# Layer two's output products with weights as the stationary side, and PSUM dealt anew

## The chip, the cores and the metric

The kernel runs on one core of a Trainium2 chip. A core has TensorE (PE: matrix products, out of SBUF into PSUM), VectorE (DVE), ScalarE (ACT), GpSimdE (POOL), and queues that start transfers (SP here, mostly). PSUM has eight banks; one holds 512 fp32 columns on 128 partitions. The metric is device time in microseconds (us), the median of several runs.

## The reference, cut to what matters

```python
# x: (4, 8, 768, 32), a: (4, 8, 768), B and C: (4, 8, 768, 16), all fp32
for c in range(nc):                         # chunked linear attention with decay
    cum = np.cumsum(la, axis=-1)            # la = log(a) of the chunk
    L = np.exp(cum[:, :, :, None] - cum[:, :, None, :]) * causal
    y_intra = ((Cc @ Bc^T) * L) @ xc
    y_inter = (Cc @ state) * np.exp(cum)
    y[chunk] = y_intra + y_inter
    state = decay_full * state + (Bc * decay_from_j)^T @ xc
x = y as (3072 tokens, 256)
h = x @ w_in                                # layer one: (3072, 256) x (256, 2048)
g = where(h > 0, h, exp(min(h, 0)) - 1)     # elu
x = g @ w_out                               # (3072, 2048) x (2048, 256)
h = x @ w_in2                               # layer two, the same sizes
g = h * tanh(softplus(h))                   # mish
out = g @ w_out2
```

## The kernel before, in words

Tokens are ordered in 32 attention tiles of 96 tokens (a chunk of 96 here, four batches in turn), and the feed-forward layers go over seven blocks of 384, 384, 512, 512, 512, 512 and 256 tokens (BL). The two layers' blocks are interleaved in one list, `order`: (1,0), (1,1), (2,0), (2,1), (1,2), (1,3), (2,2), (1,4), (2,3), (1,5), (2,4), (1,6), (2,5), (2,6), as (layer, block). A block has 16 slots, one for each 128 of the 2048 hidden features.

fp32 precision comes from splitting an operand into a high and a low fp32r part, and three products hi x hi, hi x lo, lo x hi. For h (`emit_h`) a slot has six matmuls: two halves of the 256 inputs times three, weights as the stationary side (lhsT), tokens as the moving one (rhs), so h has features on partitions and tokens in columns. ACT and DVE make g from it (`elu_1` to `elu_3`, or `mish_1`), then its parts gh and gl (`split_hi`, `split_lo`).

Layer one's second product (`emit_y1`) keeps this layout: six matmuls a slot with the block's tokens as columns, into two banks, y transposed, which is what the next layer wants. Layer two's second product (`emit_y2`) has to give rows of tokens: gh and gl are the stationary side, 128 tokens at a time, and the weights move: for each 128 tokens one matmul of 512 columns (gh with hi and lo side by side) and one of 256 (gl with hi). A block of 512 thus has four such pairs a slot and four accumulator banks. At the block's end `y2_out1` (ACT or DVE) scales the second half, `y2_out2` (DVE) adds the first, and `y2_store` writes rows of 256 floats out.

PSUM before: pool `ph` two banks (tag h), pool `pa` two banks of tag acc and two of tag accb, pool `px` two banks (tag s, attention). Tag accb has the third and fourth accumulator of layer two, attention's first outputs (`new_ys`), and the odd slots' h of layer one (`h_other`).

The order of the work on each engine comes from a planner in the kernel itself. Every piece is a `step` with the engines that can do it, a cost in us, what it depends on, and perhaps a due time `dl`. Buffers are `Ring`s: `take` gives the next turn at a buffer, and turns are used in the order in which they were taken. `run_steps` simulates the engines, picks at each moment the ready step that is due first (due times run back through what depends on a step), and emits the instructions in that order. Engines then run in order, so a step that waits holds what stands behind it on its engine, SP's transfers too. `slot_time(s)` is the time at which slot s ought to start.

Attention's steps for a tile: loads (`load_bc`, `load_c96`, `load_x`, `at_cumrow`), bf16 parts (`three_parts`) turned by a DMA transpose (`at_split_5`), the decay mask (`at_diff`, `at_mask`, `at_exp`), scores (`at_scores`), their product with the mask (`at_p`), `at_y` and `at_st` on PE, and `at_y_hi` and `at_y_lo`, which write layer one's input. The first eight tiles use PE transposes (`at_tr0`) instead.

Of the kernel before, what the change touches and what calls it, by code (L numbers as in the profile page):

```python
# [18 lines left out]
def tile_chain(  # L19
# [25 lines left out]
    FP = 2  # L45
    NP = NF // FP
# [3 lines left out]
    WB, GB, HB = 3, 3, 2  # L50
# [9 lines left out]
    px = ctx.enter_context(tc.tile_pool(name="px", bufs=2, space=bass.MemoryType.PSUM))  # L60
# [45 lines left out]
    class Need:  # L106
# [9 lines left out]
        w=Ring(WB), gh=Ring(GB), gl=Ring(GB), h=Ring(HB), acc=Ring(2), accb=Ring(2), s=Ring(2), xy=Ring(3), x=Ring(5), bc=Ring(2),  # L116
        d=Ring(2), r=Ring(1), t=Ring(1), r1=Ring(1), bw=Ring(2), o=Ring(2), stk=Ring(1),
# [219 lines left out]
    def w_hi(key, k):  # L337
        return wt[key, k][:, 0]
# [4 lines left out]

    def job_1(j, eng):
# [430 lines left out]
    def h_other(s):  # L775

        layer, c, f = at_slot(s)
        return layer == 1 and f % 2 and (f >= 5 or s >= NF and order[s // NF - 1][0] == 1)

    def emit_h(s):  # L780
# [5 lines left out]
        p, t = (pa, "accb") if h_other(s) else (ph, "h")  # L786
        h = p.tile([128, MT], F32, tag=t, name="h")[:, 0:BL[c]]
# [496 lines left out]
```

## Time and profile before

| | |
|---|---|
| median of three runs | 613.85 us (613.49 to 615.1) |
| the profiled execution | 614.17 us, span of its instructions 612.1 us |
| mean granted clock of TensorE | 0.986 |
| PE, PE weight loads | 598.7 us, 506.4 us busy |
| DVE, ACT, POOL | 433.2, 377.4, 177.6 us busy |
| instructions | 10993, of them 3876 matmuls |
| read from and written to HBM | 32.31 MB, 3.24 MB |

How to read it: a matmul's end is modelled and overlaps the next one's start, so its duration is more than what it costs; the pace is the distance between starts. The profile names for each wait the event that came last. In a row such as `h<-xyh,wi 128*128 128x512` the tile written stands ahead of the arrow, then the tiles read, the stationary size, and the moving one.

### The profile page before, as it was taken

How to read it: one execution, taken by the hardware profiler on the slowest of the kernel's cores; microseconds unless marked ns; L12 is line 12 of the kernel's file. 1: busy time of each engine (PE TensorE's matmuls, PEld its weight loads, DVE VectorE, ACT ScalarE, POOL GpSimd, SP SyncE). 2: the span in 40 equal slices, each digit the busy share in tenths (PEclk: the TensorE clock that was granted, in tenths of full speed). 3: DMA queues.
4: the chain of work that ended last, by engine and by line, in shares of the span. 5: the costliest groups of instructions: out<-in, count | busy, mean ns of one | idle time of the engine just before them, and what ended most of it. 6: DMA issues, size and time to landing. Idle time of an engine off the chain costs nothing.

```text
span 612.1 us, 10993 instructions
## 1 busy us (share of the span) xinstructions
PE 598.7 (98%) x3876; PEld 506.4 (83%) x3876; DVE 433.2 (71%) x948; ACT 377.4 (62%) x705; POOL 177.6 (29%) x238
## 2 busy tenths in 40 slices
PE   6899999999999999999999999999999999999997
PEld 5677799999987878888878888878888888988896
DVE  5899899987887888765877766767764545744454
ACT  4699999976878775554786644597544214542121
POOL 2346455222556545100544301536100000200000
PEclk9599999999999999999999999999999999999999
DMA  7799894205564543002463302533300000000010
GB/s 149 190 244 297 260 260 103 56 9 99 104 121 85 111 81 68 5 0 52 72 114 73 80 1 27 104 82 74 62 0 1 1 0 19 19 1 0 1 36 18
DMA packets 133655, 47.09 MB, mean 77 GB/s; under 512 B 116672, under 2 KB 122432, under 8 KB 133600
## 3 DMA queue, kind: packets, MB, share of 16 engines
q1 hardware_dynamic: 133488, 46.29, 34.5%
q8 instruction: 30, 0.49, 0.4%
q14 instruction: 25, 0.20, 0.1%
q10 hardware_dynamic: 112, 0.10, 0.0%
HBM read 32.31 MB, written 3.24 MB: 58 GB/s over the span
## 4 chain that ended last, share of the span: by engine, by line
PE 92%; DMA 3%; ACT 2%; DVE 1%; issue 1%; SPq 0%; ACTq 0%; DVEq 0%
PE h L789 15%; PE h L790 14%; PE h L791 14%; PE acc L883 14%; PE acc L884 7%; PE acc L852 6%; PE acc L853 6%; PE acc L854 6%; PE acc L857 4%; PE ys L716 2%; DMA t<-stk 2%; PE s L667 2%; PE s L679 1%; ACT L836 1%; PE ys L746 1%
## 5 line engine op out<-in xcount | busy, mean ns | idle before, releaser
L789 PE MATMUL h<-xyh,wi 128*128 128x512 f32 (+2 forms) x448 | 168.5, 376 | 1.0 <-ACT w L836 0.9
L790 PE MATMUL h<-xyl,wi 128*128 128x512 f32 (+2 forms) x448 | 162.2, 362 | 0.2 <-DVE xyl L733 0.2
L791 PE MATMUL h<-xyh,wi 128*128 128x512 f32 (+2 forms) x448 | 162.0, 362 | 0.0
L883 PE MATMUL acc<-wo,gh 128*128 128x512 f32 x384 | 142.5, 402 | 0.0
L832 DVE TENSOR_TENSOR gl<-w,gh 128x512 fp32r<-128x512 f32 (+2 forms) x181 | 122.5, 678 | 21.5 <-ACT gh L375 12.9
L836 ACT ACTIVATE w<-h 128x512 f32<-128x512 f32 (+2 forms) x112 | 59.4, 536 | 100.9 <-PE h L791 68.7
L884 PE MATMUL acc<-wo,gl 128*128 128x256 f32 x384 | 107.5, 280 | 0.0
L377 DVE CAST gh<-w 128x512 fp32r<-128x512 f32 (+2 forms) x114 | 47.0, 414 | 74.8 <-PE acc L883 51.2
L789 PEld LDWEIGHTS h<-xyh,wi 128*128 128x128 f32 x448 | 85.0, 190 | 17.4 <-ACT w L836 2.5
L791 PEld LDWEIGHTS h<-xyh,wi 128*128 128x128 f32 x448 | 85.0, 190 | 10.7
L790 PEld LDWEIGHTS h<-xyl,wi 128*128 128x128 f32 x448 | 85.2, 190 | 9.7 <-DVE xyl L733 0.5
L883 PEld LDWEIGHTS acc<-wo,gh 128*128 128x128 f32 x384 | 72.2, 188 | 15.5
L805 ACT ACTIVATE w<-h 128x512 f32<-128x512 f32 (+2 forms) x96 | 51.7, 540 | 51.1 <-PE h L791 37.1
L884 PEld LDWEIGHTS acc<-wo,gl 128*128 128x128 f32 x384 | 72.5, 189 | 2.2
L832 POOL TENSOR_TENSOR gl<-w,gh 128x512 fp32r<-128x512 f32 (+2 forms) x27 | 29.6, 1096 | 147.6 <-ACT gh L375 95.6
L375 ACT ACTIVATE gh<-w 128x512 fp32r<-128x512 f32 (+2 forms) x94 | 54.9, 584 | 27.8 <-PE acc L853 23.4
L852 PE MATMUL acc<-gh,wo 128*128 128x512 f32 (+2 forms) x192 | 70.2, 365 | 0.0
L854 PE MATMUL acc<-gl,wo 128*128 128x512 f32 (+2 forms) x192 | 69.6, 363 | 0.0
L853 PE MATMUL acc<-gh,wo 128*128 128x512 f32 (+2 forms) x192 | 69.6, 362 | 0.0
L813 DVE TENSOR_SCALAR w<-w 128x512 f32<-128x512 f32 (+2 forms) x74 | 30.5, 414 | 26.2 <-ACT w L805 25.2
L595 POOL TENSOR_TENSOR d<-bc,dk 32x384 f32<-32x384 f32 x28 | 27.9, 999 | 68.8 <-DVE gl L832 41.8
L821 DVE TENSOR_TENSOR w<-h,w 128x512 f32<-128x512 f32 (+2 forms) x74 | 46.6, 631 | 1.5
(102 smaller groups left out, 821.4 us busy)
## 6 DMA issues: line engine op xcount, KB each, us to landing
d<-cum_d SPq DMA_DIRECT2D x31, 288.0 KB, 3.9
raw<-in_moe_w_in_dram SPq DMA_DIRECT2D x16, 512.0 KB, 6.5
raw<-in_moe_w_out_dram SPq DMA_DIRECT2D x16, 512.0 KB, 5.9
xs<-in_x_dram SPq DMA_DIRECT2D x32, 96.0 KB, 2.9
bc<-in_C_dram SPq DMA_DIRECT2D x32, 48.0 KB, 2.4
bc<-in_B_dram SPq DMA_DIRECT2D x32, 48.0 KB, 2.7
out_dram<-o SPq DMA_DIRECT2D x15, 96.0 KB, 1.9
bc<-bc SPq DMA_DIRECT2D x84, 16.0 KB, 2.4
```

Source lines behind the costliest of these rows:

```text
L375: nc.scalar.activation(out=out, in_=in_, func=AF.Copy)
L789: nc.tensor.matmul(out=h, lhsT=hi[:, k, fs], rhs=xh[:, k, :], start=(k == 0), stop=False)
L790: nc.tensor.matmul(out=h, lhsT=hi[:, k, fs], rhs=xl[:, k, :], start=False, stop=False)
L791: nc.tensor.matmul(out=h, lhsT=lo[:, k, fs], rhs=xh[:, k, :], start=False, stop=(k == 1))
L805: nc.scalar.activation(out=new_w(s), in_=st[s][0], func=AF.Exp)
L832: alu(eng).tensor_tensor(out=gl, in0=w, in1=gh.bitcast(F32), op=ALU.subtract)
L836: nc.scalar.activation(out=new_w(s), in_=st[s][0], func=AF.Mish)
L852: nc.tensor.matmul(out=y, lhsT=hi[:, f % FP, ds], rhs=gh, start=(f == 0), stop=False)
L853: nc.tensor.matmul(out=y, lhsT=lo[:, f % FP, ds], rhs=gh, start=False, stop=False)
L854: nc.tensor.matmul(out=y, lhsT=hi[:, f % FP, ds], rhs=gl, start=False, stop=(f == NF - 1))
L883: nc.tensor.matmul(out=y, lhsT=gh[:, ts], rhs=w[:, :, f % FP, :], start=(f == 0), stop=False)
L884: nc.tensor.matmul(out=y[:, 0], lhsT=gl[:, ts], rhs=w[:, 0, f % FP, :], start=False, stop=(f == NF - 1))
```

## The change

The diff, with the changed cost figures of the planner cut to a few:

```diff
@@ -43,11 +43,12 @@
     DFF = w_in1.shape[1]
     NF = DFF // 128
     FP = 2
+    EARLY = 20.0
     NP = NF // FP
     LAG = 5
     N0 = NF
     TR0 = range(2 * NB)
-    WB, GB, HB = 3, 3, 2
+    WB, GB, HB = 3, 3, 3
 
     const = ctx.enter_context(tc.tile_pool(name="const", bufs=1))
     wpool = ctx.enter_context(tc.tile_pool(name="wpool", bufs=1))
@@ -57,7 +58,7 @@
     at = ctx.enter_context(tc.tile_pool(name="at", bufs=1))
     ph = ctx.enter_context(tc.tile_pool(name="ph", bufs=HB, space=bass.MemoryType.PSUM))
     pa = ctx.enter_context(tc.tile_pool(name="pa", bufs=2, space=bass.MemoryType.PSUM))
-    px = ctx.enter_context(tc.tile_pool(name="px", bufs=2, space=bass.MemoryType.PSUM))
+    px = ctx.enter_context(tc.tile_pool(name="px", bufs=3, space=bass.MemoryType.PSUM))
     dram = ctx.enter_context(tc.tile_pool(name="dram", bufs=1, space=bass.MemoryType.DRAM))
 
     ctx.enter_context(tc.manual_schedule())
@@ -113,8 +114,8 @@
             return iter(self.free)
 
     rings = dict(
-        w=Ring(WB), gh=Ring(GB), gl=Ring(GB), h=Ring(HB), acc=Ring(2), accb=Ring(2), s=Ring(2), xy=Ring(3), x=Ring(5), bc=Ring(2),
-        d=Ring(2), r=Ring(1), t=Ring(1), r1=Ring(1), bw=Ring(2), o=Ring(2), stk=Ring(1),
+        w=Ring(WB), gh=Ring(GB), gl=Ring(GB), h=Ring(HB), acc=Ring(2), s=Ring(3), xy=Ring(3), x=Ring(5), bc=Ring(2),
+        d=Ring(2), r=Ring(1), t=Ring(1), r1=Ring(1), bw=Ring(2), o=Ring(2), stk=Ring(1), turned=Ring(1),
     )
 
     def take(name):
@@ -341,6 +342,14 @@
         return wt[key, k][:, 1]
 
 
+    def by_rows(key, w):
+        return w.rearrange("p k f (b q) -> p (f b) k q", q=32) if key == "o2" else w
+
+    def from_raw(key, r):
+        w = r[:, :, :, 1].bitcast(F32)
+        return w.rearrange("p f (b k q) -> p (f b) k q", k=2, q=32) if key == "o2" else w
+
+
     def job_1(j, eng):
 
 
@@ -382,13 +391,14 @@
     def job_4(j, eng):
         key, k = jobs[j]
         z, n = divmod(j, NJ)
-        wt[key, k] = wpool.tile([128, 2, 2, 256], F32R, tag=f"w{z + 1}_{n}", name=f"w{key}{k}")
-        copy(eng, w_hi(key, k), raw[j][:, :, :, 1].bitcast(F32))
+        shape = [128, 2, 2, FP, 128] if key == "o2" else [128, 2, 2, 256]
+        wt[key, k] = wpool.tile(shape, F32R, tag=f"w{z + 1}_{n}", name=f"w{key}{k}")
+        copy(eng, by_rows(key, w_hi(key, k)), from_raw(key, raw[j]))
 
     def job_5(j, eng):
         key, k = jobs[j]
-        w = raw.pop(j)[:, :, :, 1].bitcast(F32)
-        alu(eng).tensor_tensor(out=w_lo(key, k), in0=w, in1=w_hi(key, k).bitcast(F32), op=ALU.subtract)
+        hi, lo = by_rows(key, w_hi(key, k)), by_rows(key, w_lo(key, k))
+        alu(eng).tensor_tensor(out=lo, in0=from_raw(key, raw.pop(j)), in1=hi.bitcast(F32), op=ALU.subtract)
 
 
     nc.scalar.preload_act_table_set("natural_log_exp_and_others")
@@ -701,10 +711,7 @@
         return res
 
     def new_ys(i):
-        if i < NB:
-            ys_t[i] = pa.tile([128, 512], F32, tag="accb", name="ys")
-        else:
-            ys_t[i] = px.tile([128, 512], F32, tag="s", name="ys")
+        ys_t[i] = px.tile([128, 512], F32, tag="s", name="ys")
 
     def at_y(i):
         c, b = divmod(i, NB)
@@ -772,19 +779,13 @@
         layer, c = order[s // NF]
         return layer, c, s % NF
 
-    def h_other(s):
-
-        layer, c, f = at_slot(s)
-        return layer == 1 and f % 2 and (f >= 5 or s >= NF and order[s // NF - 1][0] == 1)
-
     def emit_h(s):
         layer, c, f = at_slot(s)
         key = f"i{layer}"
         hi, lo = w_hi(key, f // FP), w_lo(key, f // FP)
         fs = slice((f % FP) * 128, (f % FP + 1) * 128)
         xh, xl = [t[:, :, 0:BL[c]] for t in (xT if layer == 1 else y1T)[c]]
-        p, t = (pa, "accb") if h_other(s) else (ph, "h")
-        h = p.tile([128, MT], F32, tag=t, name="h")[:, 0:BL[c]]
+        h = ph.tile([128, MT], F32, tag="h", name="h")[:, 0:BL[c]]
         for k in range(2):
             nc.tensor.matmul(out=h, lhsT=hi[:, k, fs], rhs=xh[:, k, :], start=(k == 0), stop=False)
             nc.tensor.matmul(out=h, lhsT=hi[:, k, fs], rhs=xl[:, k, :], start=False, stop=False)
@@ -870,32 +871,78 @@
             op0=ALU.mult, op1=ALU.subtract,
         )
 
+    def emit_yt(s):
+
+        _, c, f = at_slot(s)
+        if f == 0:
+            acc[2, c] = [pa.tile([128, MT], F32, tag="acc", name="acc")[:, 0:BL[c]] for _ in range(2)]
+        _, _, gh, gl = st.pop(s)
+        hi, lo = [w("o2", f // FP)[:, :, f % FP] for w in (w_hi, w_lo)]
+        for k in range(2):
+            y = acc[2, c][k]
+            nc.tensor.matmul(out=y, lhsT=hi[:, k], rhs=gh, start=(f == 0), stop=False)
+            nc.tensor.matmul(out=y, lhsT=lo[:, k], rhs=gh, start=False, stop=False)
+            nc.tensor.matmul(out=y, lhsT=hi[:, k], rhs=gl, start=False, stop=(f == NF - 1))
+
+    def yt_turn(c, k):
+        if k == 0:
+            tl["t", c] = at.tile([128, MT // 32, 64], F32, tag="raw", name="turned")
+        nc.vector.transpose(
+            out=tl["t", c][:, 0:BL[c] // 32, 32 * k:32 * k + 32],
+            in_=acc[2, c][k].rearrange("p (g t) -> p g t", t=32),
+        )
+
+    def yt_scale(c, eng):
+        t = tl["t", c][:, 0:BL[c] // 32]
+        if eng == A:
+            nc.scalar.activation(out=t, in_=t, func=AF.Copy, scale=1.0 / WS)
+        else:
+            nc.vector.tensor_scalar_mul(t, t, 1.0 / WS)
+
+    def yt_store(c, p):
+        tile_, i = divmod(BS[c] + p, T)
+        n = min(T - i, BL[c] - p)
+        r0 = (tile_ % NB) * S + (tile_ // NB) * T + i
+        for g in range(n // 32):
+            r = r0 + 32 * g
+            nc.sync.dma_start(
+                out=out[r:r + 32, :].rearrange("t (b e) -> b t e", b=4), in_=tl["t", c][:, p // 32 + g]
+            )
+
     def emit_y2(s, k):
         _, c, f = at_slot(s)
         n = min(128, BL[c] - 128 * k)
         if f == 0:
 
-            acc[2, c, k] = pa.tile([128, 2, DM], F32, tag="acc" if k < 2 else "accb", name="acc")[0:n]
+            acc[2, c, k] = pa.tile([128, 2, DM], F32, tag="acc", name="acc")[0:n]
         _, _, gh, gl = st[s]
         w = wt["o2", f // FP]
         y = acc[2, c, k]
         ts = slice(k * 128, k * 128 + n)
-        nc.tensor.matmul(out=y, lhsT=gh[:, ts], rhs=w[:, :, f % FP, :], start=(f == 0), stop=False)
-        nc.tensor.matmul(out=y[:, 0], lhsT=gl[:, ts], rhs=w[:, 0, f % FP, :], start=False, stop=(f == NF - 1))
+        yk = y.rearrange("p z (k e) -> p z k e", k=2)
+        nc.tensor.matmul(out=yk, lhsT=gh[:, ts], rhs=w[:, :, :, f % FP, :], start=(f == 0), stop=False)
+        nc.tensor.matmul(
+            out=yk[:, 0], lhsT=gl[:, ts], rhs=w[:, 0, :, f % FP, :], start=False, stop=(f == NF - 1)
+        )
+
+    def in_rows(y, o):
+        return y.rearrange("p (k b q) -> p k b q", k=2, b=4), o.rearrange("p (b k q) -> p k b q", k=2, b=4)
 
     def y2_out1(c, k, eng):
         n = min(128, BL[c] - 128 * k)
         o = tl["o", c, k] = at.tile([128, DM], F32, tag="o", name="o", bufs=2)[0:n]
+        a, b = in_rows(acc[2, c, k][:, 1], o)
         if eng == V:
-            nc.vector.tensor_scalar_mul(o, acc[2, c, k][:, 1], 1.0 / WS)
-        else:
-            nc.scalar.activation(out=o, in_=acc[2, c, k][:, 1], func=AF.Copy, scale=1.0 / WS)
+            nc.vector.tensor_scalar_mul(b, a, 1.0 / WS)
+        else:
+            nc.scalar.activation(out=b, in_=a, func=AF.Copy, scale=1.0 / WS)
 
     def y2_out2(c, k):
-        o = tl["o", c, k]
-        nc.vector.scalar_tensor_tensor(
-            out=o, in0=acc[2, c, k][:, 0], scalar=1.0 / WS, in1=o, op0=ALU.mult, op1=ALU.add
-        )
+        a, b = in_rows(acc[2, c, k][:, 0], tl["o", c, k])
+        for j in range(2):
+            nc.vector.scalar_tensor_tensor(
+                out=b[:, j], in0=a[:, j], scalar=1.0 / WS, in1=b[:, j], op0=ALU.mult, op1=ALU.add
+            )
 
     def y2_store(c, k):
         o = tl["o", c, k]
...
@@ -984,6 +1031,7 @@
                   dl=slot_time(2 * NF + k * FP) + 10.0 if j >= NJ else 1e9)
         lock.update((q4, q5))
         rf.append(q5)
+        raw_f = rf
         w_ready[key, k] = [q4, q5]
         LW.append(q0)
         if key == "o1":
@@ -1012,17 +1060,18 @@
         for q in pieces(i):
             w = q[3] / T
             YHI[i][q[0]] = step((A, 0.14 + 0.14 * w, lambda q=q: at_y_hi(i, *q)), y, xy_f["x", q[0]][1])
-            YLO[i][q[0]] = step((V, 0.10 + 0.2 * w, lambda q=q: at_y_lo(i, *q)), YHI[i][q[0]])
+            dl = slot_time(order.index((1, q[0])) * NF) - EARLY if i >= 14 else 1e9
+            YLO[i][q[0]] = step((V, 0.10 + 0.2 * w, lambda q=q: at_y_lo(i, *q)), YHI[i][q[0]], dl=dl)
         return list(YHI[i].values()) + list(YLO[i].values())
 
     def three_parts(i, need):
 
         sf, sn = take("stk")
         rf, rn = take("r1")
-        a1 = step((A, 0.88, lambda: at_split_1(i)), need, sn)
-        a2 = step(alt(lambda e: at_split_2(i, e), (V, 0.50), (G, 0.50)), a1, rn)
-        a3 = step((A, 0.68, lambda: at_split_3(i)), a2)
-        a4 = step(alt(lambda e: at_split_4(i, e), (V, 0.50), (G, 0.50)), a3)
+        a1 = step((A, 0.84, lambda: at_split_1(i)), need, sn)
+        a2 = step(alt(lambda e: at_split_2(i, e), (V, 0.46), (G, 0.82)), a1, rn)
+        a3 = step((A, 0.63, lambda: at_split_3(i)), a2)
+        a4 = step(alt(lambda e: at_split_4(i, e), (V, 0.46), (G, 0.82)), a3)
         tf, tn = take("t")
         a5 = step((DQ, 0.62, lambda: at_split_5(i), 2.0, True), a4, tn)
         lock.update((a2, a4))
@@ -1034,17 +1083,18 @@
         pz = []
         for z in range(2):
             pf, pn = take("s")
-            sc = step((PE, 0.4 if cold else 0.38, lambda z=z: at_scores(i, z)), a5, pn)
+            sc = step((PE, 0.19, lambda z=z: at_scores(i, z)), a5, pn)
             pz.append(step((V, 0.47, lambda z=z: at_p(i, z)), sc, ex, r_n))
             pf.append(pz[-1])
             tf.append(sc)
         return pz
 
+    tr_s = [take("s") for _ in range(NB)]
     for i in range(NB):
         cold = i in TR0
         if cold:
-            tf, tn = take("s")
-            tr = step((PE, 0.64, lambda i=i: at_tr0(i)), s_lc[i], s_lb[i], s_c2, tn)
+            tf, tn = tr_s[i]
+            tr = step((PE, 0.5, lambda i=i: at_tr0(i)), s_lc[i], s_lb[i], s_c2, tn)
             gf, gn = take("g" + "hl"[i // 2])
             cp = step(alt(lambda e, i=i: at_tr0_out(i, e), (A, 0.37), (V, 0.47)), tr, gn)
             tf.append(cp)
...
@@ -1102,11 +1152,11 @@
         BW[i] = (bf, bw)
         xf[i].append(y)
 
-    af, an = take("accb")
+    af, an = take("s")
     acc_f = {0: [take("acc"), take("acc")]}
     for i in range(NB):
         bf, bw = BW[i]
-        sp_ = step((PE, 0.19, lambda i=i: at_st(i)), bw, LX[i], an, SO.get(i - 1, []))
+        sp_ = step((PE, 0.37, lambda i=i: at_st(i)), bw, LX[i], an, SO.get(i - 1, []))
         SO[i] = step((V, 0.95, lambda i=i: at_st_out(i)), sp_, LX[i + NB])
         bf.append(sp_)
         xf[i].append(sp_)
...
@@ -1178,12 +1228,12 @@
         blk = s // NF
         u = BL[c] / 384
         if f == 0 and s:
-            acc_f[blk] = [take("acc" if k < 2 else "accb") for k in range(2 if layer == 1 else NK[c])]
+            acc_f[blk] = [take("acc") for _ in range(2)]
         if layer == 1:
             src = [p[c] for i in range(tiles) for p in (YHI[i], YLO[i]) if c in p]
         else:
             src = EV[1, c]
-        hf, hn = take("accb" if h_other(s) else "h")
+        hf, hn = take("h")
         n = BL[c]
         pe = 6 * (0.0135 + n / 2395)
         h = HS[s] = step((PE, 1.95 * u if s < 2 else pe, lambda s=s: emit_h(s)), src, w_ready[f"i{layer}", f // FP], hn,
@@ -1235,6 +1285,25 @@
                     q = step((V, ct, lambda c=c, k=k: y1_lo(c, k)), p)
                     EV[1, c] += [p, q]
                     acc_f[blk][k][0].extend([p, q])
+        elif c < NBL - 1:
+            y = YS[s] = step((PE, pe, lambda s=s: emit_yt(s)), ydep, an, YS.get(s - 1, []), dl=ydl)
+            gf.append(y)
+            lf.append(y)
+            if f == NF - 1:
+                tf, tn = take("turned")
+                if c == 0:
+                    tn = raw_f
+                turned = []
+                for k in range(2):
+                    turned.append(step((V, ct, lambda c=c, k=k: yt_turn(c, k)), y, tn))
+                    acc_f[blk][k][0].append(turned[-1])
+                o = step(alt(lambda e, c=c: yt_scale(c, e), (A, 0.12 + n * 0.0016), (V, 0.09 + n * 0.00116)), turned)
+                lock.add(o)
+                p = 0
+                while p < n:
+                    m = min(T - (BS[c] + p) % T, n - p)
+                    tf.append(step((DQ, 0.5 * (m // 32), lambda c=c, p=p: yt_store(c, p), 0.3), o))
+                    p += m
         else:
             prev = YS.get(s - 1, [])
             YS[s] = []
```

In words: for layer two's blocks but the last (`c < NBL - 1`), `emit_yt` makes y transposed as layer one does, six matmuls a slot into two banks. `yt_turn` lets DVE transpose 32x32 blocks of a bank into an SBUF tile, `yt_scale` scales that tile on ACT or DVE, and `yt_store` writes 32 tokens with each DMA, in runs of 64 floats. So that the blocks come out in order, the output weights of layer two are written to SBUF with their columns permuted (`by_rows`, `from_raw`, in `job_4` and `job_5`); the last block still uses `emit_y2`, with views that undo the permutation, and `y2_out2` is two instructions. PSUM is dealt three banks for h, three for attention (tag s, which now has attention's first outputs too), two accumulators (tag acc); tag accb and `h_other` go. The low part of attention's output (`at_y_lo`) has a due time 20 us ahead of its block's first slot, for tiles from 14 on. The turns at tag s of the first four `at_tr0` are taken ahead of the loop. Costs in the planner change, at the places shown and at some 15 others of the same kind (PE's small products, POOL's passes).

## Rows read from the trace of the kernel before

**Rows 1.** Page, part 1: busy us, share of span, instructions.

```profile
PE 598.7 (98%) x3876; PEld 506.4 (83%) x3876; DVE 433.2 (71%) x948; ACT 377.4 (62%) x705; POOL 177.6 (29%) x238
```

**Rows 2.** Page, part 4: chain that ended last, shares by engine.

```profile
PE 92%; DMA 3%; ACT 2%; DVE 1%; issue 1%; SPq 0%; ACTq 0%; DVEq 0%
```

**Rows 3.** Busy us (instructions) of PE, PEld, DVE, ACT, POOL by stretch; clock, DMA share, GB/s.

```profile
20.00:30.00 10.00, 8.20 (x76) 6.43 (x68) 8.93 (x25) 5.98 (x12) 3.19 (x4) 0.50 0.65 191
...
80.00:90.00 10.00, 10.00 (x58) 9.87 (x58) 8.97 (x16) 9.93 (x22) 5.59 (x7) 1.00 1.09 228
```

**Rows 4.** Timeline, layer one, block of 512: start, duration, engine, line, instruction.

```profile
247.99 0.39 PE L789 MATMUL h<-xyh,wi 128*128 128x512 f32 x1
...
269.75 0.39 PE L789 MATMUL h<-xyh,wi 128*128 128x512 f32 x1
```

**Rows 5.** Timeline, layer two, block of 512, no attention beside it.

```profile
552.42 0.40 PE L789 MATMUL h<-xyh,wi 128*128 128x512 f32 x1
...
560.79 0.40 PE L789 MATMUL h<-xyh,wi 128*128 128x512 f32 x1
...
562.17 0.39 PE L883 MATMUL acc<-wo,gh 128*128 128x512 f32 x1
...
563.57 0.40 PE L789 MATMUL h<-xyh,wi 128*128 128x512 f32 x1
...
574.72 0.40 PE L789 MATMUL h<-xyh,wi 128*128 128x512 f32 x1
```

**Rows 6.** Timeline, layer two, block of 384.

```profile
124.87 0.34 PE L789 MATMUL h<-xyh,wi 128*128 128x384 f32 x1
...
135.28 0.34 PE L789 MATMUL h<-xyh,wi 128*128 128x384 f32 x1
```

**Rows 7.** Waits of PE: for what, us in total, times, longest.

```profile
PE h L789 <- ACT w L836: 0.9, 3, 0.5
...
PE s L679 <- DMA t<-stk: 0.5, 2, 0.3
...
PE h L790 <- DVE xyl L733: 0.2, 1, 0.2
```

**Rows 8.** Timeline, end of layer one's sixth block, all engines.

```profile
475.58 1.28 ACT L864 ACTIVATE xyh<-acc 128x512 fp32r<-128x512 f32 x2 [1.44 <-PE acc L854]
...
476.07 0.39 PE L789 MATMUL h<-xyh,wi 128*128 128x512 f32 x1
...
477.25 1.28 DVE L868 SCALAR_TENSOR_TENSOR xyl<-acc,xyh 128x512 fp32r<-128x512 f32 x2
...
478.79 0.39 PE L883 MATMUL acc<-wo,gh 128*128 128x512 f32 x1
```

**Rows 9.** Line 617, the only VectorE transpose: duration ns min/median/max.

```profile
L617 DVE STREAM_TRANSPOSE r<-d x28: 564/574/577, 34.0 to 505.6; 32x384 f32<-32x384 f32 x28
```

**Rows 10.** Line 868: duration ns min/median/max, first and last start, forms.

```profile
L868 DVE SCALAR_TENSOR_TENSOR xyl<-acc,xyh x14: 415/679/684, 81.5 to 547.7; 128x512 fp32r<-128x512 f32 x8, 128x384 fp32r<-128x384 f32 x4, 128x256 fp32r<-128x256 f32 x2
```

**Rows 11.** Timeline, last instructions of ScalarE and VectorE.

```profile
607.29 0.73 ACT L892 ACTIVATE o<-acc 128x256 f32<-128x256 f32 x2 [2.64 <-PE acc L884]
...
607.70 0.77 DVE L896 SCALAR_TENSOR_TENSOR o<-acc,o 128x256 f32<-128x256 f32 x2 [1.33 <-ACT o L892]
```

**Rows 12.** Groups by form: ScalarE's copies of output weights.

```profile
L375 ACT ACTIVATE wo<-raw 128x512 fp32r<-128x512 f32 x13 | 8.6, 671 | 0.1
```

**Rows 13.** Timeline of PE, first tiles of attention, first h.

```profile
14.97 0.87 PE L716 MATMUL ys<-r,xs 96*32 96x96 f32 x16
...
17.09 0.89 PE L629 MATMUL p_tr<-ident,bc 96*112 96x96 f32 x4
...
25.71 0.69 PE L789 MATMUL h<-xyh,wi 128*128 128x384 f32 x1
```

**Rows 14.** DMA issues: KB each, us from issue to landing.

```profile
bc<-in_C_dram SPq DMA_DIRECT2D x32, 48.0 KB, 2.4
...
t<-stk SPq DMA_TRANSPOSE x24, 3.9
```

More of the change, by code (lines that the diff above doesn't have):

```diff
@@ L948, in tile_chain @@
         af, an = take("acc")
-        s_d4 = step((PE, 0.15, lambda t=t: decays_4(t)), s_d1, an)
+        s_d4 = step((PE, 0.77, lambda t=t: decays_4(t)), s_d1, an)
         s_d5.append(step(alt(lambda e, t=t: decays_5(t, e), (V, 0.47), (A, 0.37)), s_d4))
@@ L954, in tile_chain @@
     af, an = take("acc")
-    s_d6 = step((PE, 0.1, decays_6), s_d5, s_c2, an)
+    s_d6 = step((PE, 0.5, decays_6), s_d5, s_c2, an)
     s_d7 = step(alt(decays_7, (V, 0.2), (A, 0.2)), s_d6)
@@ L1072, in tile_chain @@
                 f = lambda e, i=i, g=g: at_diff(i, g * H // 2, (g + 1) * H // 2, e)
-                dd.append(step(alt(f, (G, 1.0), (V, 0.47)), lc, s_q6))
+                dd.append(step(alt(f, (G, 0.88), (V, 0.47)), lc, s_q6))
                 lock.add(dd[-1])
-        mk = step((G, 0.95, lambda i=i: at_mask(i)), dd)
+        mk = step((G, 0.93, lambda i=i: at_mask(i)), dd)
         ex = step((A, 0.78, lambda i=i: at_exp(i)), mk)
@@ L1103, in tile_chain @@
         xf[i].append(y)
-    af, an = take("accb")
+    af, an = take("s")
     acc_f = {0: [take("acc"), take("acc")]}
@@ L1124, in tile_chain @@
             pf, pn = take("s")
-            tr = step((PE, 0.6, lambda i=i: at_tr0(i)), lb, pn)
+            tr = step((PE, 0.45, lambda i=i: at_tr0(i)), lb, pn)
             tf, tn = take("t")
@@ L1133, in tile_chain @@
             f = lambda e, i=i, g=g: at_diff(i, g * H // 2, (g + 1) * H // 2, e)
-            dd.append(step(alt(f, (G, 1.0), (V, 0.47)), lc, s_q6))
+            dd.append(step(alt(f, (G, 0.88), (V, 0.47)), lc, s_q6))
             lock.add(dd[-1])
-        mk = step((G, 0.95, lambda i=i: at_mask(i)), dd)
+        mk = step((G, 0.93, lambda i=i: at_mask(i)), dd)
         ex = step((A, 0.78, lambda i=i: at_exp(i)), mk)
         table[ex] = "exp"
-        cs = step((G, 0.95, lambda i=i: at_cs(i)), l96, lc, s_d5)
+        cs = step((G, 0.92, lambda i=i: at_cs(i)), l96, lc, s_d5)
         r_f, r_n = take("r")
-        rc = step((V, 0.56, lambda i=i: at_rc(i)), cs, r_n)
+        rc = step((V, 0.6, lambda i=i: at_rc(i)), cs, r_n)
         rc2 = step(alt(lambda e, i=i: at_rc2(i, e), (V, 0.37), (A, 0.52)), rc)
@@ L1153, in tile_chain @@
                 two = [take("s"), take("s")]
-                sc = step((PE, 0.65, lambda i=i, z=z: at_scores0(i, z)), a2, [n for _, n in two])
+                sc = step((PE, 0.55, lambda i=i, z=z: at_scores0(i, z)), a2, [n for _, n in two])
                 tf.append(sc)
@@ L1163, in tile_chain @@
         if c + 1 < NCH:
-            y = step((PE, 0.65, lambda i=i: (at_y(i), at_st(i))), pz, rc, rc2, LX[i], pn, SO[i - NB], b1, b2)
+            y = step((PE, 0.67, lambda i=i: (at_y(i), at_st(i))), pz, rc, rc2, LX[i], pn, SO[i - NB], b1, b2)
             SO[i] = step((V, 0.95, lambda i=i: at_st_out(i)), y, LX[i + NB])
```

## The prediction

> **What bounds the kernel now.** I read the busy shares first: TensorE (PE) is busy 598.7 of 612.1 us, VectorE (DVE) 433.2, ScalarE (ACT) 377.4 [rows 1]. A busy PE alone proves little, so the chain of waits comes next: 92% of it is PE work, 3% DMA, 2% ACT [rows 2]. From the first product of the feed-forward layers at 25.7 us [rows 13] to the end, PE has something to issue nearly always, and what it waits for by name is small: 0.9 us for ACT to free a bank of h, 0.5 us for attention's DMA transposes, 0.2 us for attention's last low part [rows 7]. So the end moves by what PE's own stream costs, then by the few waits in it, then by the tail. Work taken from DVE, ACT or the queues alone moves nothing.
>
> The third view is therefore the pace of PE's stream, start to start (durations overlap, so the starts are what counts). In a layer-one block of 512 tokens, eight slots (a slot is one 128-wide slice of d_ff: the products that make h, and those that use it) run from 247.99 to 269.75, which is 2.720 us each [rows 4]. In a layer-two block of the same size, with the same number of columns, eight slots run from 552.42 to 574.72, which is 2.788 us each [rows 5]. The reader is to see where that extra 0.068 us lies: the six h matmuls take 560.79 to 562.17, 1.38 us, against 1.36 for half a layer-one slot, and the four pairs 512 + 256 take 562.17 to 563.57, 1.40 us [rows 5].
>
> **The change part by part.** The sum is made against the profiled execution, 614.17 us (span 612.1, 2.1 around it); it lies 0.32 above the median 613.85, so 0.3 is taken off at the end.
>
> *Last products turned.* For blocks of layer two but the last, eight matmuls a slot (four of 512 columns, four of 256) become six of 512, with weights as the stationary side, which is what layer one does already. Columns stay: 4 x 768 = 6 x 512 = 3072. What goes is the irregular stream, so I take layer one's slot for the new one: 4 blocks of 512 x 16 slots x 0.068 = -4.3 us. The bounds: 0 if the new slot keeps 2.788 us, and -4.8 if every matmul took 0.226 us (12 x 0.226 = 2.712). I choose the layer-one row, since the new stream has its shapes, operands and order. Blocks of 384: five slots of layer two took 124.87 to 135.28, 2.082 us [rows 6], and 58 matmuls of layer one's 384-token block fill 10 us [rows 3], 0.172 to 0.174 us each, 2.07 to 2.09 for twelve. Nothing is won there.
>
> Here a page speaks against the gain. The Trainium skill (TensorE: Matmul & The Clock Gate, "Back-to-back issue gap") gives the warm gap as N/2.4 ns plus about 2.5 ns for each matmul; by it the slot goes from 2.595 to 2.590 us, and 64 slots give an estimated 0.3 us. The trace disagrees with the page on both slots: 2.788 and 2.720 us, and the difference is many times larger than two issue costs.
>
> *PSUM dealt 3/3/2.* Layer two had two banks for h, now three; layer one had two and a share of the other pair, now three. PE's idle 0.9 us for ACT at h [rows 7] are three waits for such a bank. Each costs about 0.17 us more than its idle time shows, since a matmul's modelled end (0.40 us) lies 0.17 behind the next start (0.23 us on). 0.9 + 3 x 0.17 = -1.4 us if all three go. Bounds 0 and -1.4; I take -1.4, as a third bank gives ACT a whole slot more. What is late next is DVE's release of gh and gl, three buffers each as before.
>
> *Accumulators.* Layer two kept its sums in four banks, now two, and one pair must be empty before the next block's first sum starts. After a block's last y, DVE turns two banks one behind the other. No row shows a 128x512 transpose out of PSUM: the 32x384 one takes 574 ns [rows 9], by columns 0.77 us for 512; a plain DVE pass of 512 columns out of PSUM takes 0.68 us [rows 10]. I take 0.75, the transposing row, so 1.5 us, with some 0.3 for signals and up to 0.7 behind a gl already begun on DVE: 1.8 to 2.5 us. Behind a waiting first y in PE's queue stand the next h and all that follows. What hides it are h products put ahead: at the end of layer one's sixth block the drain (ACT 1.28 us from 475.58, DVE 1.28 from 477.25, so to 478.53) passes under two h slots issued from 476.07, and the next sum starts at 478.79 with no idle row at either matmul [rows 8]. That drain is longer than the new one, so 0 us; without cover 1.8 us for each of six ends, 10.8 us. Scaling (one pass over 128x1024) and stores run behind the turn, and the next turn of that tile is a whole block away.
>
> *Tail.* The last block keeps the old products, but y2_out2 is two instructions where it was one. Line 868 gives 679 ns at 512 columns and 415 at 256 [rows 10], so 1.03 ns a column, and by that 0.28 us for 128. The last two sums take 0.77 us together now [rows 11]; four pieces take 1.1. +0.3 us, bounds 0 and +0.5.
>
> *Weights in row order.* Hi and lo of layer two's output weights are written through a permuted view with runs of 32: eight tiles. A copy takes 671 ns now [rows 12]. If the view doubled it, ACT or DVE would do 8 x 0.67 = 5.4 us more, in a stretch where ACT is busy 9.93 of 10 us [rows 3] though PE is the one without a gap. I take 0 (columns count, not runs), bounds 0 and +2.
>
> *Start.* The four first tr0 steps now take their banks ahead of any y, so the first y, at 14.97, may not begin before tile 3's transposes, which ran at 17.09 [rows 13]: up to 2.9 us later for that y, but layer one needs all four y before it starts at 25.71, and PE has the same work between. The stretch 20 to 30 runs at a granted clock of 0.50 (the 1.2 GHz level) with PE busy 8.20 [rows 3], so an order that fills or opens gaps moves it either way: 0, bounds -2 and +2.
>
> *Deadline for attention, new durations.* Tiles from 14 on are wanted 20 us earlier, so their chains move forward, into layer-one blocks. Each moves its DMAs on SP too; the stores also change, from one per run of rows to one per 32 tokens, 88 in all for six blocks, at some 0.5 us of SP each. A store waiting for the scaling holds the loads behind it on SP. Best case, the waits for transposes and for the low part go: 0.5 + 0.2 + 3 x 0.17 = -1.2 us. Worst case, one in three of 18 tiles meets a late transpose (median 3.9 us to land [rows 14]) at 0.25 + 0.17 us: +2.5. I take 0. Short runs as such don't frighten here: loads whose runs are 64 bytes land in 2.4 us [rows 14], and new stores have runs of 256.
>
> Sum: -4.3 - 1.4 + 0.3 = -5.4; 614.17 - 5.4 = 608.8; less 0.3 to the median: **608.5 us**.
>
> **The rivals.**
> *Columns alone count.* The slot stays 2.788 us, as the columns are the same, and only the bank waits go: 613.85 - 1.4 + 0.3 = 612.8. For it: the column counts, and h itself is slower in layer two (1.38 against 1.36), which could lie in what the other engines do there. Against it: the layer-one rows.
> *Attention gains as well.* Earlier chains end the waits for them: 608.5 - 1.2 = 607.3, and a fuller start could take it to 606.5. For it: [rows 7]. Against it: these waits are short and few.
> *Attention pulled into new waits.* Urgent scores stand in PE's queue before their transposes have landed: 608.5 + 2.5 = 611.0, with SP slowed by 88 stores to 611.5.
> *Bare block ends (slower).* The two turns on DVE are not covered, because PE's order puts the next first y right behind them: 608.5 + 10.8 = 619.3 in full. It cancels the whole gain from about 0.9 us an end on (5.4 / 6). For it: two banks instead of four, and both turns on one engine. Against it: [rows 8], the same drain hidden.
>
> **How the numbers follow.** Forecast 0.52, columns alone 0.13, attention gains 0.15, new waits 0.11, bare ends 0.09. About 0.3% (1.84 us) is what a measurement of this kernel can tell from no change: faster is below 612.0, slower above 615.7. Faster: 0.51 + 0.15 + 0.07 + 0.02 = 0.75. Slower: 0.07 of bare ends and 0.01 of new waits, 0.08. Same: the rest, 0.17. The forecast's own range is 606 to 611; down to 605.0 it takes in the attention gain, up to 612.9 the new waits and most of columns alone, leaving out bare ends and a worse start.
>
> **What would show it.** Right: layer two's slots of 512 at 2.72 us and its h at 1.36; no PE wait for ACT's w at h; DVE transposes of 128x512 near 0.75 us with h products running through them and no gap before the next block's first sum; the first h near 25.7 us; the last DVE pieces ending 0.3 us later behind the last matmul. Wrong: slots of 2.79 (columns alone); idle PE ahead of a block's first sum (bare ends); more than two waits of scores for t (new waits); a first h over 2 us away from 25.7.

## The result, and the profile after

The changed kernel takes 608.38 us (median of four runs, 608.07 to 609.11), the one before 614.28 beside it; the ratio is 0.9906 (95% interval 0.9888 to 0.9923). The profiled execution took 608.07 us with a span of 606.4.

The page's busy shares (part 1) and the chain that ended last (part 4), after, against [rows 1, 2]:

```profile
PE 593.1 (98%) x3748; PEld 502.6 (83%) x3748; DVE 426.0 (70%) x931; ACT 384.8 (63%) x707; POOL 175.7 (29%) x233
...
PE 95%; DVE 2%; DMA 1%; ACT 0%; issue 0%; POOL 0%; DVEq 0%; POOLq 0%
```

128 matmuls fewer, 5.6 us less of busy PE, and PE's share of the chain up from 92% to 95%: the kernel is more purely bound by PE than it was. The pace of a layer-two block of 512 (the timeline of PE, first h matmul of slots eight apart), against [rows 5]:

```profile
547.29 0.39 PE L790 MATMUL h<-xyh,wi 128*128 128x512 f32 x1
...
569.05 0.39 PE L790 MATMUL h<-xyh,wi 128*128 128x512 f32 x1
```

21.76 us for eight slots, 2.720 each, as layer one had [rows 4]; before it was 2.788. What PE waits for by name, after, against [rows 7] (all rows):

```profile
PE p_cr L656 <- DVE cum L458: 4.4, 1, 4.4
PE s L677 <- DVE r L683: 1.9, 1, 1.9
PE ys L753 <- DVE xs L763: 1.3, 1, 1.3
PE s L677 <- DVE dec L386: 0.4, 1, 0.4
PE ys L723 <- DVE r L683: 0.3, 1, 0.3
```

All five lie ahead of the first h, and none of the three waits of [rows 7] is left. The start is later (PE's timeline), against [rows 13]:

```profile
15.46 1.48 PE L677 MATMUL s<-f32t 16*96 16x96 f32 x14 [1.94 <-DVE r L683]
...
17.69 0.87 PE L723 MATMUL ys<-r,xs 96*32 96x96 f32 x16
...
27.03 0.44 PE L753 MATMUL ys<-xs,bw 96*32 96x64 f32 x8 [1.29 <-DVE xs L763]
27.40 0.69 PE L790 MATMUL h<-xyh,wi 128*128 128x384 f32 x1
```

The first y starts at 17.69 (14.97 before), the first h at 27.40 (25.71). A block end, with both turns, then the first sum of the last block (timeline, all engines), against [rows 8]:

```profile
581.04 1.41 DVE L890 STREAM_TRANSPOSE turned<-acc 128x512 f32<-128x512 f32 x2 [0.74 <-PE acc L885]
...
581.30 0.39 PE L885 MATMUL acc<-gl,wo 128*128 128x512 f32 x1
581.53 0.28 PE L790 MATMUL h<-xyh,wi 128*128 128x256 f32 x1
...
582.96 0.40 PE L923 MATMUL acc<-wo,gh 128*128 128x512 f32 x1
```

The turns end and the banks are empty at 582.45 (581.04 + 1.41). PE makes two slots of h meanwhile, 12 matmuls from 581.53 without a gap, and starts the next sum at 582.96. Single pieces, against [rows 9, 11, 12]: the turn (duration ns min/median/max), a copy of output weights (busy us, mean ns), and the tail (timeline):

```profile
L890 DVE STREAM_TRANSPOSE turned<-acc x12: 535/674/718, 154.7 to 581.7; 128x512 f32<-128x512 f32 x8, 128x384 f32<-128x384 f32 x4
...
L384 ACT ACTIVATE wo<-raw 128x512 fp32r<-128x512 f32 x13 | 8.9, 682 | 0.4 <-DVE wi L401 0.3
...
601.29 0.73 ACT L938 ACTIVATE o<-acc 128x256 f32<-128x256 f32 x2 [2.63 <-PE acc L924]
...
601.71 0.88 DVE L943 SCALAR_TENSOR_TENSOR o<-acc,o 128x128 f32<-128x128 f32 x4 [1.33 <-ACT o L938]
```

### The profile page after: what moved, and what is told of

It reads as the page before. It is cut to its first block, busy times and chain, and to the rows that moved or that the text cites. A ratio compares the mean times of both kernels' runs of the same rounds, so it can differ in the third digit from the quotient of the medians.

```text
span 606.4 us, 10757 instructions
## 1 busy us (share of the span) xinstructions
PE 593.1 (98%) x3748; PEld 502.6 (83%) x3748; DVE 426.0 (70%) x931; ACT 384.8 (63%) x707; POOL 175.7 (29%) x233
## 4 chain that ended last, share of the span: by engine, by line
PE 95%; DVE 2%; DMA 1%; ACT 0%; issue 0%; POOL 0%; DVEq 0%; POOLq 0%
PE h L790 15%; PE h L792 14%; PE h L791 14%; PE acc L883 7%; PE acc L884 7%; PE acc L885 7%; PE acc L853 6%; PE acc L854 6%; PE acc L855 6%; PE acc L858 4%; PE ys L723 2%; PE s L689 2%; PE acc L923 1%; PE s L677 1%; DMA t<-stk 1%; PE acc L924 1%
## 5 line engine op out<-in xcount | busy, mean ns | idle before, releaser
L833 DVE TENSOR_TENSOR gl<-w,gh 128x512 fp32r<-128x512 f32 (+2 forms) x176 | 117.5, 670 | 21.0 <-ACT gh L384 11.9
L833 POOL TENSOR_TENSOR gl<-w,gh 128x512 fp32r<-128x512 f32 (+2 forms) x32 | 36.4, 1138 | 230.0 <-ACT gh L384 124.7
L386 DVE CAST gh<-w 128x512 fp32r<-128x512 f32 (+2 forms) x107 | 42.4, 396 | 75.4 <-PE acc L884 52.6
L384 ACT ACTIVATE gh<-w 128x512 fp32r<-128x512 f32 (+2 forms) x101 | 57.7, 571 | 28.1 <-PE acc L854 19.6
L883 PE MATMUL acc<-gh,wo 128*128 128x512 f32 (+1 forms) x192 | 72.4, 377 | 0.0
L884 PE MATMUL acc<-gh,wo 128*128 128x512 f32 (+1 forms) x192 | 71.5, 372 | 0.0
L885 PE MATMUL acc<-gl,wo 128*128 128x512 f32 (+1 forms) x192 | 71.4, 372 | 0.0
L822 DVE TENSOR_TENSOR w<-h,w 128x512 f32<-128x512 f32 (+2 forms) x72 | 44.3, 615 | 1.5
L576 POOL TENSOR_SCALAR_AFFINE_SELECT d<-d 96x768 f32<-96x768 f32 x32 | 28.9, 903 | 42.2 <-DVE gh L386 16.6
L853 PEld LDWEIGHTS acc<-gh,wo 128*128 128x128 f32 x192 | 36.2, 189 | 5.3
```

The costliest lines, as they stand in the source:

```text
L384: nc.scalar.activation(out=out, in_=in_, func=AF.Copy)
L833: alu(eng).tensor_tensor(out=gl, in0=w, in1=gh.bitcast(F32), op=ALU.subtract)
L853: nc.tensor.matmul(out=y, lhsT=hi[:, f % FP, ds], rhs=gh, start=(f == 0), stop=False)
L883: nc.tensor.matmul(out=y, lhsT=hi[:, k], rhs=gh, start=(f == 0), stop=False)
L884: nc.tensor.matmul(out=y, lhsT=lo[:, k], rhs=gh, start=False, stop=False)
L885: nc.tensor.matmul(out=y, lhsT=hi[:, k], rhs=gl, start=False, stop=(f == NF - 1))
```

## The experiments

Each was timed beside the kernel before. Ratios are to it; the changed kernel's own is 0.9906. Diffs are against the changed kernel unless said otherwise.

**The products alone.** In the kernel before: `emit_yt`, `yt_turn`, `yt_scale`, `yt_store`, the permuted weights, and nothing else.

```diff
-    WB, GB, HB = 3, 3, 3
+    WB, GB, HB = 3, 3, 2                        # px back to two banks, accb back, old costs
+        p, t = (pa, "accb") if h_other(s) else (ph, "h")
-            dl = slot_time(order.index((1, q[0])) * NF) - EARLY if i >= 14 else 1e9
+            dl = 1e9
```

> The turned products of layer two (with the permuted weights, the turn, the scaling and the stores) put into the kernel before: PSUM as before (two h, two acc, two accb, two s), planner's costs as before, no due time for attention. Theory (the regular stream): slots of 512 in layer two fall from 2.788 to 2.72 us, so -4.3 us, tail +0.3: 610.3 us (609.3 to 611.2); first h near 25.7 us; bank waits at h as before. Rival (the planner's new order makes the gain, columns alone count): 613.4 to 614.6, slots still near 2.79.

Measured: 607.8 us (607.56 to 608.02), 0.9896 (0.9882 to 0.991). The whole gain is here, and 2.5 us more than expected; slots at 2.72, first h at 25.80. The surplus has a row: bank waits were expected as before, and of PE's waits after the first h one remains, with two banks for layer two's h as before.

```profile
PE h L798 <- ACT w L845: 0.2, 1, 0.2
```

So in this order the waits of h for a bank went with the new products, without a third bank. Adding up PE's stream, from the start of each output product of layer two to the start of PE's next matmul (waits included), gives 140.8 us in the kernel before and 135.2 here: 5.6 of the 6.0 us by which the span is shorter.

**Without attention's due time.**

```diff
-            dl = slot_time(order.index((1, q[0])) * NF) - EARLY if i >= 14 else 1e9
+            dl = 1e9
```

> The changed kernel without attention's due time (1e9 in its place). Theory: attention's place in the order is worth at most its waits, so 608.4 to 609.2, with a wait of scores for t or of h for the low part back in PE's stream. Rival (the due time makes the gain): 610 or more. Rival (the due time costs): 607.5 or less.

Measured: 614.32 us (613.2 to 615.21), 1.0005 (0.9995 to 1.0015). The whole gain is gone, though the slots still run at 2.72. The windows (us, then busy us of PE, PEld, DVE, ACT, POOL, clock, DMA share, GB/s) and PE's longest wait after the start show one place:

```profile
230.00:240.00 10.00, 6.45 (x60) 4.72 (x53) 7.65 (x20) 5.94 (x14) 4.83 (x8) 0.95 0.55 115
240.00:250.00 10.00, 10.00 (x41) 8.15 (x41) 6.47 (x14) 7.41 (x14) 5.47 (x7) 0.88 0.44 73
...
PE s L689 <- DMA t<-stk: 2.4, 1, 2.4
```

PE runs out of products at the change from block (1,2) to (1,3), because attention's last tiles for (1,3) come late; it stands 3.55 us, and then the granted clock is 0.95 and 0.88 (part of the stretch at the 1.2 GHz level), where the changed kernel has 1.00. By these rows the lower clock costs another 1.7 us (0.05 and 0.12 of 10 us each, an estimate), so this one place has some 5.2 of the 5.5 us by which this trace is longer.

**Old planner costs.**

```diff
-        s_d4 = step((PE, 0.77, lambda t=t: decays_4(t)), s_d1, an)
+        s_d4 = step((PE, 0.15, lambda t=t: decays_4(t)), s_d1, an)
...
```

> The changed kernel with all the planner's costs as before (durations not as traced). The first h, at 27.4 us with the new costs and 25.7 before, should be back near 25.7 if the costs made the start later. If the start's 1.7 us are carried to the end: 606.7. If layer one's first blocks take them up (another limit there): 608.0 to 608.8. Rival (the new costs make part of the gain elsewhere): 610 or more.

Measured: 608.59 us (608.28 to 609.07), 0.9911 (0.9899 to 0.9924): the same as the changed kernel. The first h came at 27.05 us, so the costs are not what makes the start late, and they give nothing.

**Layer two with two banks of h.**

```diff
+    def h_third(s):
...
+        return layer == 1 and f % 3 == 2
...
+        p, t = (po, "ho") if h_third(s) else (ph, "h")
```

> The changed kernel, but the third h bank serves only layer one's slots 2, 5, 8, 11 and 14: layer two's h has two banks as before. Theory (third bank ends waits at h): waits of h for ACT's w back, about three, 609.4 to 610.2. Rival (the third bank does nothing): 608.2 to 608.8. A fixed bank for a slot can cost layer one something too: its own waits of h for DVE's w would show that.

Measured: 612.88 us (612.21 to 613.98), 0.9982 (0.9973 to 0.999). Slower than both theories had it, and not by the wait they named:

```profile
PE s L690 <- DMA t<-stk: 1.0, 1, 1.0
PE acc L889 <- DVE turned L896: 0.9, 1, 0.9
PE acc L890 <- DVE wo L402: 0.4, 1, 0.4
PE h L796 <- ACT w L843: 0.4, 1, 0.4
```

0.4 us are waits for a bank of h, and 0.9 us for an accumulator that DVE is still turning: at that block end the drain isn't covered, though in the changed kernel it is. These four rows are 2.7 of the 4.7 us by which the span is longer; another 1.3 lie behind the last matmul. Why this deal makes them is open, since the banks and the order changed together.

**The first y in a bank of h.**

```diff
-        new_ys(i)
+        new_ys(i, *((ph, "h") if i < NB else ()))
...
-            tf, tn = tr_s[i]
+            tf, tn = take("s")
...
```

> The changed kernel, but attention's first four y go to banks of h (not of attention), the first four tr0 take their banks in turn in the loop as before, and the planner's costs of the two decay products (p_e, p_d) are as before. Theory (the start's 1.7 us come from y's sharing attention's three banks, so that a y waits for the last tr0): first h back at 25.7 to 26.2 us, and 606.4 to 607.4 in all if PE carries the start to the end. Rival (layer one's first block takes it up, since other engines set its pace): first h earlier, but 608.0 to 608.8.

Measured: 608.03 us (607.35 to 610.27), 0.9908 (0.9892 to 0.9925), as the changed kernel. First h at 26.66, but the third block starts at 106.3 against 106.1 there: nothing of it reaches the end, as the rival had it. PE's waits move to y (four, 3.0 us, for DVE's r), and two new ones stand behind the first h, for other engines as the rival said:

```profile
PE s L677 <- ACT f32t L384: 0.8, 1, 0.8
...
PE h L790 <- DVE g L822: 0.6, 1, 0.6
```

The 0.7 us is also no more than the first h moves between traces: in two kernels with the changed kernel's start untouched it came at 26.71 (every turn twice) and 28.04 (halves).

**The products in halves.**

```diff
+            parts = [slice(0, n // 2), slice(n // 2, n)] if 0 < f < NF - 1 else [slice(0, n)]
+            for u in parts:
-            nc.tensor.matmul(out=y, lhsT=hi[:, k], rhs=gh, start=(f == 0), stop=False)
+                nc.tensor.matmul(out=y[:, u], lhsT=hi[:, k], rhs=gh[:, u], start=(f == 0), stop=False)
...
```

> The changed kernel with layer two's turned products in halves of 256 (or 192) columns in slots 1 to 14 of a block: the same columns, 6 more matmuls a slot, 504 in all. Rows of before: a matmul of 512 costs 0.227 us, one of 256 0.120, so a split costs 0.013 us. Theory (each matmul has a fixed cost besides its columns): +6.7 us, and up to 0.9 more for h behind narrow matmuls: 614.5 to 616.5. Rival (columns alone count): 608.0 to 609.5. Rival (only the mix of widths in the stream costs, not the number): 609 to 611.

Measured: 621.48 us (620.61 to 621.98), 1.0118 (1.0103 to 1.0133): +13.1 us for no column more, above all three ranges. By starts, the 256-column halves cost 0.120 us each, as expected; the 192-column ones 0.1125, where 0.5 x 0.173 + 0.0065 = 0.093 was expected, so layer two's two blocks of 384 lost 7.6 us and its blocks of 512 lost 3.8. The six h matmuls behind the narrow ones take 1.388 us in the blocks of 512, not 1.360, which is 1.6 more. Neither columns alone nor the mixture alone sets the time: the number of matmuls counts.

**Every turn twice.**

```diff
+        for _ in range(2):
             nc.vector.transpose(
```

> The changed kernel with every DVE turn done twice, and the planner told nothing of it: each of six block ends gets 1.35 us more on DVE (two turns of 0.67) before the accumulators are free. Theory (the drain lies under h products put ahead, with room): under 0.5 us at an end, 608.2 to 611. Rival (the drain is just covered, or bare): every us shows, 614 to 617.

Measured: 609.48 us (608.81 to 610.11), 0.9924 (0.9909 to 0.9939): +1.1 us over the changed kernel for 8 us more on DVE at block ends. One wait on it shows:

```profile
PE acc L853 <- DVE turned L891: 0.3, 1, 0.3
```

The drain is covered: in the changed kernel's trace the next sum starts 0.5 to 1.6 us behind the drain's end, over 1 us at four of the six ends.

**The products alone, with the due time.**

```diff
# against the products alone
-            dl = 1e9
+            dl = slot_time(order.index((1, q[0])) * NF) - EARLY if i >= 14 else 1e9
```

> The turned products in the kernel before (as in the run with them alone: old PSUM deal, old costs), plus attention's due time for tiles from 14 on. Theory (the due time only repairs what three banks for attention and two accumulators do to the order): 607.3 to 608.3, as without it. Rival (the due time is worth something in itself): 605.5 to 607.0. Rival (it costs something): 609 or more.

Measured: 614.3 us (613.99 to 615.31), 1.0008 (0.9999 to 1.0016). The same line that is worth 6 us in the changed kernel costs 6.5 here, with slots at 2.72 again. PE's waits:

```profile
PE h L798 <- ACT w L845: 3.0, 7, 0.9
...
PE s L689 <- DVE xyl L743: 0.6, 1, 0.6
PE h L798 <- DVE w L828: 0.4, 1, 0.4
...
PE s L689 <- DMA t<-stk: 0.4, 1, 0.4
```

These are 4.4 us, where the products alone had 0.2. The last rival was right: the due time costs something here.

**Four banks for h, two for attention, without and with the due time.**

```diff
# against the products alone, and against those with the due time
-    WB, GB, HB = 3, 3, 2
+    WB, GB, HB = 3, 3, 4                        # accb gone; the first four y and the state in h
```

> The turned products alone (old costs, no due time), with PSUM dealt four banks for h, two accumulators, two for attention; attention's first four y and the first state products use banks of h. Theory (PE's stream sets the end, the third and later bank of h only removes waits): the waits of h left in the run with the products alone are small (0.2 us), so 607.0 to 608.3. Rival (a better deal gives more): under 607. Rival (any new order can cost us of waits): 609 or more.

> The same with four banks of h, and attention's due time on. With two banks for layer two's h that due time cost 6.5 us, seven waits of h for ACT's w among them. Theory (those waits were bank waits: ACT with attention's exp work beside it releases h late): four banks end them, 606.0 to 608.5. Rival (the due time packs attention too tightly for ACT and DVE whatever the banks): 611 to 614.5.

Measured: 613.49 us (611.42 to 614.85), 0.9986 (0.9977 to 0.9995), without it; 616.19 us (615.02 to 618.53), 1.0045 (1.0031 to 1.0059), with it. More banks for h did not bring the gain back: the first is in the range of its last rival (609 or more), the second above every range. With the due time no wait of h for ACT's w is left in the list, so those were bank waits, but other waits stand there:

```profile
PE ys L726 <- DVE r L683: 4.2, 4, 1.7
PE acc L861 <- DVE raw L376: 0.8, 1, 0.8
PE acc L856 <- DVE turned L893: 0.7, 1, 0.7
PE ys L756 <- DVE xs L766: 0.7, 1, 0.7
PE s L689 <- DVE xyl L743: 0.6, 1, 0.6
PE ys L726 <- ACT r L384: 0.6, 1, 0.6
```

The largest, y for DVE's r, is 4.2 us without the due time too, so it belongs to this deal, where the first four y use banks of h; the third row is again a drain that isn't covered. Without the due time the clock adds to the loss in the trace, of an execution of 614.85 us (windows as above):

```profile
30.00:40.00 10.00, 8.45 (x69) 5.95 (x67) 9.35 (x27) 8.66 (x17) 7.23 (x10) 0.67 0.76 203
40.00:50.00 10.00, 10.00 (x54) 8.37 (x53) 7.47 (x15) 7.83 (x16) 3.87 (x6) 0.85 1.08 264
```

PE stands 1.55 us here, and the granted clock is 0.67 and 0.85, where the products alone have 0.92 and 1.00.

**The planner's part alone.** Old products, old deal, new costs and due time.

```diff
# against the kernel before
+            dl = slot_time(order.index((1, q[0])) * NF) - EARLY if i >= 14 else 1e9
-        s_d4 = step((PE, 0.15, lambda t=t: decays_4(t)), s_d1, an)
+        s_d4 = step((PE, 0.77, lambda t=t: decays_4(t)), s_d1, an)
...
```

> The kernel before with the new planner costs and attention's due time only: old products, old PSUM deal. Theory (the gain is in the products' stream): no gain, 613 to 616, perhaps slower, as the due time with two banks of h was. Rival (the planner's part gives some of the 6 us by itself): 611.5 or less.

Measured: 615.14 us (613.56 to 620.47), 1.0028 (1.0008 to 1.0048): no gain by itself. Two of its twelve executions took 620 us, the others 613.6 to 615.5, so a loss isn't clear either.

**A try at a better version.**

```diff
+    def ys_in(i):
+        return "ho" if i in (0, 2) else "so"
...
+        p, t = (po, "ho") if s % 3 == 2 else (ph, "h")
...
```

> A try at a better version: the changed kernel with its 3/3/2 deal, but one bank of h (every third slot) and one of attention (for y and state) are named banks of their own, so that the first four y alternate between these two and need not wait behind the four tr0; the costs of p_e and p_d as before, due time on. Theory (the products' stream with the start of the kernel before and no waits later): first h at 25.7 to 26.2 us, 606.3 to 607.5 in all. Rival (the start is made up by the first two blocks anyway): 607.8 to 608.8. Rival (any new order may bring waits in the attention stretch, as the runs with four banks for h did): 610 to 614.

Measured: 610.59 us (609.83 to 611.2), 0.9944 (0.9931 to 0.9958). The first h came at 24.39 us, 3.0 ahead of the changed kernel's, and the median lies 2.2 us above that kernel's, as the last rival had it: PE's waits behind the first h come to 2.5 us, against 0.1 there. No version ran that is clear of the changed kernel; the products alone (0.9896) and it (0.9906) can't be told apart.

## Why the prediction was right, point by point

- **The pace (-4.3 us): right, and shown.** Slots of 512 in layer two, where no attention stands among them, run at 2.72 us in every kernel with the turned products whole, at 2.79 in the two without. In the changed kernel h in these blocks is at layer one's pace too. Of the rivals, "columns alone" is out by this row and by the halves. What "the irregular stream" is can be sized from the starts (0.227 us at 512 columns, 0.120 at 256): ten and four of them come to 2.75 us, so by this estimate the two further matmuls of a slot cost about 0.03 of the 0.068 us, and the mixture of widths the other 0.04. The Trainium skill's gap of N/2.4 + 2.5 ns (TensorE: Matmul & The Clock Gate, "Back-to-back issue gap") would have given 0.3 us for the stretch and 1.3 us for the 504 matmuls of the halves (an estimate by that page); the runs show 4.3 and 13. That section gives the formula for a matmul by itself and says that in a stream of weight loads and matmuls both set the spacing, so it doesn't speak against the gain, though the prediction has it so.
- **Blocks of 384 (0): right.** The steady slot is 12 matmuls of 0.173 us there, as layer one's.
- **Bank waits (-1.4): the size was right, the cause was not.** All three waits went, but they went with two banks for layer two's h as well (products alone: 0.2 us left). With another order they return (due time on, two banks: 3.0 us). A third bank makes layer two less sensitive to the order; that it earned the 1.4 us here isn't shown.
- **Accumulators (0): right.** Two turns of 0.70 us (0.75 assumed) under two slots of h, and twice the turn cost 1.1 us in six ends. "Bare block ends" is out for this kernel; in other orders single ends were bare, for 0.9 us (layer two with two banks of h) and 0.7 us (four banks with the due time).
- **Tail (+0.3): the sign was right, the size +0.11.** Four pieces took 0.88 us, not 1.1.
- **Weights in row order (0): right.** A copy takes 682 ns against 671.
- **Start (0): wrong in the place, right at the end.** The first y was late as feared (2.7 us) and the first h by 1.7. What I had as "PE has the same work between" didn't hold: PE waited 3.9 us for DVE there in all. But kernels whose first h came 0.7 us (y in h's bank) and 3.0 us earlier (own banks) ended no earlier, and both have new waits behind the first h (1.4 and 2.5 us).
- **Due time and new costs (0): the step that was mis-sized, and hid it by luck.** The costs are worth nothing (0.9911 against 0.9906). The due time is worth 6 us in this deal of PSUM, and costs 6.5 in the old one. I priced it by the waits it could end in the trace of before (1.2 us) or bring (2.5), as if the rest of the order stayed. It doesn't: each edit to banks or due times makes the planner place attention anew, and what that costs ranged over 8 us (607.8 to 616.2) among kernels with the same stream of products. The mechanism of the rival "new waits" is real: without the due time it shows at one place, with 3.55 us of idle PE and a lower clock behind it.

So the total, 608.4 for 608.5, is the pace and the waits that left with it, in an order that happened to bring no others. The sum over spans: -4.3 (slots), -1.4 (bank waits), -1.2 (other waits of [rows 7]), +1.7 (first h), +0.2 (from the last matmul's start to the end) is -5.0; measured -5.8. The 0.8 left is not put down to a cause by any run. One cost that the list of waits doesn't have can be read from PE's starts, here in the kernel before:

```profile
283.35 0.52 PE L679 MATMUL s<-t 96*96 96x96 bf16 x8
283.70 0.47 PE L852 MATMUL acc<-gh,wo 128*128 128x512 f32 x1
...
285.16 0.39 PE L789 MATMUL h<-xyh,wi 128*128 128x512 f32 x1
```

Behind a group of attention's small matmuls the next six of 512 columns take 1.46 us, not 1.36. Behind the first h, PE returns from attention to the feed-forward products 64 times in the kernel before, 50 times in the changed one and 65 times in the products alone. At 0.1 us each, an estimate, the 14 returns saved are 1.4 us, more than the 0.8 left; and 15 returns are 1.5 us, about what the products alone have ahead by a first h 1.6 us earlier, which would explain why the two end alike. No run changed the returns alone.

What stays open: why the greedy planner finds the good order with one pair of settings and not with its neighbours. It would take runs with single steps moved by hand.

## What to carry to other kernels

Where an engine is busy all the time, read its pace from start to start in two steady stretches with equal columns: a difference there comes back in every slot, though waits elsewhere can eat it, as in four kernels here that had the new pace and hardly any of the gain. Prefer few, equally wide matmuls. Where a planner orders the work, a due time or a bank is not an edit with a price of its own: after each such edit look for the one place where the busiest engine runs dry, and judge parts by runs of each part alone, and in the deal that they will stand in, since here one due time is worth 5.9 us in one deal of PSUM and costs 6.5 in the other.

## What the runs showed that I had not expected

A matmul of 192 columns costs 0.1125 us from start to start and one of 256 costs 0.120, against 0.227 for 512: from 256 to 192 columns the time hardly falls any more. The halves' rows (by form: busy us, mean ns) have mean durations of 283 and 274 ns; the last row is a weight load (PEld):

```profile
L886 PE MATMUL acc<-gh,wo 128*128 128x256 f32 x224 | 63.4, 283 | 0.0
...
L887 PE MATMUL acc<-gh,wo 128*128 128x192 f32 x112 | 30.7, 274 | 0.0
...
L887 PEld LDWEIGHTS acc<-gh,wo 128*128 128x128 f32 x360 | 68.7, 191 | 2.4
```

Each matmul here has a weight load of its own. The Trainium skill has a rule of about the right size for it (the same page, "LDWEIGHTS (loading the stationary operand)": columns of the stationary side over 1.2 GHz, for 128 of them an estimated 107 ns). The trace doesn't confirm it, since it lists these loads with 191 ns each, overlapping the matmuls, and no run here took a load away; what sets the 0.1125 us stays open.
